# Sixteen half chunks of attention values by products of rounded halves, and the second routing search held back

## The chip, the cores and the metric

The kernel runs on one core of a Trainium2 chip. A core has a matrix engine (TensorE, PE in the rows; its weight loads are PEld), a vector engine (VectorE, DVE), a scalar engine (ScalarE, ACT), GpSimd (POOL), SyncE (SP, which only issues transfers) and 16 DMA engines. Each engine runs its own instructions in order and waits for others by semaphores. The metric is device time in microseconds (us), median of the runs; lower is better.

## The reference

A channel attention gives 20,224 tokens of 256 features, and a mixture of 8 experts with a fixed capacity works on them. Cut to what matters:

```python
qn = q / (np.linalg.norm(q, axis=1, keepdims=True) + 1e-06)      # q, k, v: 4 x 5056 x 256
kn = k / (np.linalg.norm(k, axis=1, keepdims=True) + 1e-06)
s = kn.transpose(0, 2, 1) @ qn / tau                             # 256 x 256 for each of 4 batches
a = softmax(s)                                                   # rows
x = (v @ a).reshape(20224, 256)                                  # attention values
logits = x @ w_gate                                              # 20224 x 8
for idx in np.argsort(-logits.flatten()):                        # greedy: best pairs first
    tok, e = idx // 8, idx % 8
    if assigned[tok] < 0 and counts[e] < 2528:
        assigned[tok] = e; counts[e] += 1
for e in range(8):
    out[assigned == e] = np.maximum(x[assigned == e] @ w1[e], 0) @ w2[e]
```

## The kernel before

**Stages.** First the scores of the four batches (`scores`), beside the values v @ a of batch 0 (`value`) and part of batch 1. From about 220 us PE works through the remaining values ("late" values): 13 chunks of 1024 tokens, listed in `TODO`, each in four pairs of 128 tokens (`pair` at L1494, `x_tiles` at L236). Values go through PSUM tile `px`, are evicted by ACT into `xs` (L245) and stored to the DRAM table `x_d` by a transfer that ACT issues (L251, `store_x`). Then come eight phases, one for each expert: `layer1` (L1399, tile `ph`, products at L1425) and `layer2` (L1442, tile `py`, products at L1459) over chunks of up to 512 tokens, whose rows were gathered from `x_d` by indirect transfers of POOL (L1198, tile `xg`) and turned by PE into `pt` (`turn`, `turn_both`) or by a longer way over DVE and DRAM (`stage`).

**Two kinds of product.** A late value is a matmul of full float32: per pair, 2 tiles x 2 halves of the contraction = 4 matmuls of 256 columns. Layers 1 and 2 and the values of batch 0 use three products of rounded halves instead: with v = vH + vL and a = aH + aL (H rounded to float32r, L the rest), vH aH + vH aL + vL aH, so 3 matmuls for one, in a format that PE takes in one pass.

**The routing.** Which tokens go to an expert is found by a search on DVE: `route(p, R)` prepares a 16-bit key of each token (m at L549, f at L574, the expert's one-hot `oh` at L580), then 8 rounds narrow a threshold. In a round DVE compares (`ge`, L650), PE counts (20 small matmuls, L615, and one at L628), DVE reduces, and ACT copies counts (`eq`, L643). Then `compact` and `listed` make the list of token rows: PE tests (L855, tile `pi`), ACT and DVE count them (`junk` at L873, `junkv` at L889), and DVE makes addresses (from `at`, L983, to `src`, L936). For phase 0 the list comes in two pieces, of 4 and 16 columns of 128 tokens. `("ei", 0)` in the code is the point where the expert is known (`ei`, L766), `("idx", 0)` the point where its list is complete.

**What sets the order.** From L1484 on the order is written by a planner (`Order`, L1029): the main program calls `tick` after each PE instruction with its estimated time, and `hook` then puts in DVE, PE and ACT steps of the searches where its model says that they are ready. Engines follow that order strictly. `plan` (L1119) starts the search of phase p when `("routed", p - 1)` is set, which for p = 1 lies before the list of phase 0 is complete. `pairs[:-LATE]` runs beside the first search, `until(("idx", 0))` lets the planner's clock run on (it puts nothing on PE), and the last 6 pairs stand behind it; before the sixth, four gathers and `turn_both` (L1376) bring in the first two columns of phase 0. The weights of phase 0 are loaded into `ub` when `ei` is known (L1163) and split into halves in eight pieces, `split_piece`: ACT makes the high half (L1176), DVE the low one (L1179), into the four buffers `ua`. Those four also hold values' inputs (`HOMES`); seven more chunks lie in `vr`.

## Time and profile before

| | us |
|---|---|
| time, median of 3 runs (1235.07 to 1235.74) | 1235.32 |
| the profiled execution's own time | 1232.93 |
| its span in the trace | 1231.2 |
| PE busy (98% of the span) | 1208.6 |
| DVE busy (71%) | 872.8 |
| ACT busy (46%) | 560.3 |
| POOL busy (32%) | 395.0 |
| last stretch of the late values, 307 to 322.5: PE busy of 15.5 | 15.50 |
| the list of phase 0, 290 to 307: DVE busy of 17 | 16.02 |

The profiled execution took 1232.93 us, 2.4 us less than the median. Busy time is what the profiler saw an engine execute; matmuls overlap, so a busy PE is one that has work, and what a matmul costs is read from the distance between equal steps rather than from its own duration. The timeline gives start and duration of instructions, and in brackets how long the engine had been idle and which instruction ended that wait.

### The profile page before, as it was taken

Reading aid. Unit: us, or ns where it says so; the run is one execution under the profiler, and the core shown is the slowest. Engines: PE = TensorE matmul, PEld = TensorE weight load, DVE = VectorE, ACT = ScalarE, POOL = GpSimd, SP = SyncE. Lnnn points to the kernel's source line nnn. Section 1 sums busy time; section 2 is a strip of 40 time slices with the busy share of each in tenths; the row PEclk is TensorE's granted clock in tenths of the full one; section 3 lists DMA queues with packets and bytes.
Section 4 is the critical chain, followed back from the end, with each engine's and each line's share of the span. In section 5 each row is a group of like instructions: output and inputs, shape, how many; then the busy total and the mean of one; then the engine's idle time right before and its main releaser. Section 6 shows DMA issues by size and latency. Waiting matters only on the chain.

```text
span 1231.2 us, 23522 instructions
## 1 busy us (share of the span) xinstructions
PE 1208.6 (98%) x8797; PEld 1101.6 (89%) x8797; DVE 872.8 (71%) x2414; ACT 560.3 (46%) x1301; POOL 395.0 (32%) x663
## 2 busy tenths in 40 slices
PE   7999999999999999999999999999999999999998
PEld 6889977888889999898989999989989998998998
DVE  6788695879689888979878987888766335435431
ACT  6567652235344453435343554463366435334331
POOL 1000000000353452254424443443353345344322
PEclk9999999999999999999999999999999999999999
DMA  8998985235323331332412252342243234322311
GB/s 304 357 398 310 395 322 188 103 123 204 124 95 118 113 101 66 133 95 85 148 63 87 85 184 74 116 137 90 71 148 132 78 112 166 111 81 95 115 65 34
DMA packets 67699, 179.37 MB, mean 146 GB/s; under 512 B 11008, under 2 KB 33920, under 8 KB 62976
## 3 DMA queue, kind: packets, MB, share of 16 engines
q1 hardware_dynamic: 40528, 98.58, 22.3%
q0 software_dynamic: 17664, 58.22, 14.5%
q10 hardware_dynamic: 9392, 21.06, 4.4%
q8 instruction: 69, 1.13, 0.4%
q14 instruction: 46, 0.38, 0.1%
HBM read 118.06 MB, written 59.77 MB: 144 GB/s over the span
## 4 chain that ended last, share of the span: by engine, by line
PE 81%; DVE 9%; issue 5%; POOL 2%; ACT 1%; DMA 1%; POOLq 0%; SPq 0%; DVEq 0%; ACTq 0%
PE py L1459 29%; PE ph L1425 28%; PE s L320 9%; PE px L241 8%; PE px L284 2%; PE pc L615 2%; POOL out_dram L1470 1%; PE px L432 1%; DVE hL L1434 1%; DMA xg<-x_d,src 1%; DVE acc_q L330 1%; DVE acc_k L330 1%; DVE xL L1293 1%; DMA ua<-in_q_dram 1%; DVE m L549 1%
## 5 line engine op out<-in xcount | busy, mean ns | idle before, releaser
L1459 PE MATMUL py<-ua,hH 128*128 128x256 f32 (+1 forms) x2560 | 439.2, 277 | 0.0
L1425 PE MATMUL ph<-xH,ua 128*128 128x512 f32 (+3 forms) x1312 | 395.7, 377 | 4.1 <-DVE hL L1434 3.8
L1459 PEld LDWEIGHTS py<-ua,hH 128*128 128x128 f32 (+1 forms) x2560 | 389.8, 191 | 1.4
L1459 PE MATMUL py<-ua,hL 128*128 128x256 f32 (+1 forms) x1280 | 353.1, 276 | 0.0
L1434 DVE SCALAR_TENSOR_TENSOR hL<-ph,hH 128x512 fp32r<-128x512 f32 (+3 forms) x328 | 217.7, 666 | 138.2 <-ACT hH L1429 137.5
L1429 ACT ACTIVATE hH<-ph 128x512 fp32r<-128x512 f32 (+3 forms) x328 | 190.9, 583 | 199.5 <-PE ph L1425 193.9
L1425 PEld LDWEIGHTS ph<-xH,ua 128*128 128x128 f32 x1312 | 246.3, 190 | 35.4 <-DVE hL L1434 6.9
L1470 POOL DMA_INDIRECT out_dram<-y,idx x160 | 161.8, 1011 | 305.3 <-ACT y L1468 256.2
L1425 PE MATMUL ph<-xL,ua 128*128 128x512 f32 (+3 forms) x656 | 246.9, 376 | 1.8 <-DVE xL L1293 1.8
L1459 PEld LDWEIGHTS py<-ua,hL 128*128 128x128 f32 (+1 forms) x1280 | 244.2, 191 | 0.0
L1198 POOL DMA_INDIRECT xg<-x_d,src x160 | 160.4, 1003 | 99.6 <-issue 46.9
L1468 ACT ACTIVATE y<-py 128x256 f32<-128x256 f32 (+1 forms) x160 | 61.5, 385 | 272.4 <-PE py L1459 220.8
L320 PE MATMUL s<-ua 128*128 128x256 f32 (+1 forms) x640 | 144.8, 386 | 6.9 <-DMA ua<-in_q_dram 6.9
L320 PEld LDWEIGHTS s<-ua 128*128 128x128 f32 (+1 forms) x640 | 121.8, 193 | 26.4 <-issue 10.6
L1425 PEld LDWEIGHTS ph<-xL,ua 128*128 128x128 f32 x656 | 124.9, 190 | 17.6 <-DVE xL L1293 3.9
L329 ACT ACTIVATE sq<-ua 128x1024 f32<-128x1024 f32 (+1 forms) x80 | 76.3, 970 | 49.8 <-DVE acc_k L330 16.4
L1293 DVE TENSOR_TENSOR xL<-xT,xH 128x256 fp32r<-128x256 f32 (+1 forms) x140 | 51.8, 417 | 36.6 <-ACT xH L1289 35.9
L1209 POOL COPY spacer<-hH 1x1 f32<-1x1 f32 x129 | 27.4, 212 | 154.5 <-ACT hH L1429 135.9
L245 ACT ACTIVATE xs<-px 128x512 f32<-128x512 f32 x60 | 35.8, 597 | 66.8 <-PE px L241 66.6
L350 POOL TENSOR_SCALAR ny<-ny 128x4 f32<-128x4 f32 x4 | 2.0, 505 | 182.3 <-ACT ny L349 182.3
L1179 DVE TENSOR_TENSOR ua<-ub,ua 128x512 fp32r<-128x512 f32 x64 | 47.2, 744 | 11.3 <-ACT ua L1176 9.9
L1289 ACT ACTIVATE xH<-xT 128x256 fp32r<-128x256 f32 (+1 forms) x140 | 54.2, 454 | 1.3 <-DMA xT<-via 1.3
(317 smaller groups left out, 1399.8 us busy)
## 6 DMA issues: line engine op xcount, KB each, us to landing
x_d<-xs ACTq DMA_DIRECT2D x40, 512.0 KB, 3.0
ua<-in_k_dram SPq DMA_DIRECT2D x35, 512.0 KB, 6.9
ua<-in_q_dram SPq DMA_DIRECT2D x35, 512.0 KB, 7.6
via<-xs SPq DMA_DIRECT2D x34, 512.0 KB, 2.8
xT<-via SPq DMA_DIRECT2D x136, 128.0 KB, 2.8
vr<-in_vt_dram SPq DMA_DIRECT2D x14, 1024.0 KB, 9.2
ua<-in_vt_dram SPq DMA_DIRECT2D x4, 1024.0 KB, 4.8
xg<-x_d,src POOLq DMA_INDIRECT x160
```

What stands on the lines that cost most here:

```text
L241: mm = PE.matmul(px[:, i * C:i * C + width], lhsT=vs[b, c][:, kb, t + i, :], rhs=a_f[b][:, kb, 0:width], start=(kb == 0), stop=(kb == 1))
L320: newest[0] = PE.matmul(sb[:, ib * C:(ib + 1) * C], lhsT=kt[:np_, t, ib * 128:(ib + 1) * 128], rhs=qt[:np_, t, :], start=(first and t == 0 ...
L329: S.activation(sq[:n, t0:t1], t_[:n, t0:t1], AF.Square)
L1198: P.indirect_dma_start(out=xg[:n, i, :], out_offset=None, in_=rows, in_offset=bass.IndirectOffsetOnAxis(ap=routed[p]["src", col][:n, col:c ...
L1289: S.activation(hi[:, a], rows[:, a], AF.Copy)
L1293: V.tensor_tensor(lo[:, a], rows[:, a], hi[:, a].bitcast(F32), op=OP.subtract)
L1425: PE.matmul(ph[:, 0:nt], lhsT=l[:, w], rhs=in_turn(x_, kb, nt).rearrange("p a m -> p m a"), start=(i == 0), stop=(i == 5))
L1429: S.activation(hH[:, fb, 0:nt], ph[:, 0:nt], AF.Relu)
L1434: V.scalar_tensor_tensor(hL[:, fb, 0:nt], ph[:, 0:nt], 0.0, hH[:, fb, 0:nt].bitcast(F32), op0=OP.max, op1=OP.subtract)
L1459: PE.matmul(py[:n, 0:C], lhsT=l[:, fb, tk], rhs=w, start=(j == 0), stop=(j == 23))
L1468: S.activation(y[:n], py[:n, 0:C], AF.Copy)
L1470: sd = P.indirect_dma_start(out=out, out_offset=bass.IndirectOffsetOnAxis(ap=routed[p]["idx", col][:n, col:col + 1], axis=0), in_=y[:n], i ...
```

## The change

The late chunks are divided. Five stay plain (`PLAIN`: (3,0) to (3,4)). Eight (`CLOVEN`: (2,4), (1,2) to (1,4), (2,0) to (2,3)) are worked in 16 half chunks of 512 tokens by the three products of rounded halves. For each half chunk `cleave` has ACT write -vH into the low tile (128 x 1024), POOL issue a transfer that reads v again from DRAM and adds it there (giving vL = v - vH), and ACT write vH. The halves of `a` for batches 1 and 2 are made once, the high one by ACT, the low one by POOL. `x_tiles_cut` then issues 12 matmuls for a pair. `TURNS` orders half chunks: F is two plain pairs, C one cloven half chunk; 14 plain pairs and all 32 cloven ones stand ahead of `until(("idx", 0))`, the last 6 plain ones behind it as before. `PLACES` and `BEHIND` say which freed buffer a half chunk takes and which turns must have passed. In `plan`, the search of phase 1 now waits for `("idx", 0)`. Line numbers behind the insertion are 43 to 44 higher in the changed kernel (L615 becomes L658, L549 becomes L592, L1425 becomes L1469).

```diff
@@ -67,7 +67,11 @@
 GATES_AT = (3, 3)
 FIRST_LAT = 3000
 HOMES = {(1, 0): "ub", (1, 1): "ub", (2, 4): "ua", (3, 0): "ua", (3, 1): "ua", (3, 2): "ua", (3, 3): "late", (3, 4): "late"}
-TODO = ((2, 4), (3, 0), (3, 1), (3, 2), (1, 2), (1, 3), (1, 4), (2, 0), (2, 1), (2, 2), (2, 3), (3, 3), (3, 4))
+PLAIN = ((3, 0), (3, 1), (3, 2), (3, 3), (3, 4))
+CLOVEN = ((2, 4), (1, 2), (1, 3), (1, 4), (2, 0), (2, 1), (2, 2), (2, 3))
+TURNS = "FFCFCFCCFCFCCCFCCCCCCCC"
+PLACES = ("ub", "ub", "ua", "ua", "vr", "ub", "vr", "ub", "vr", "ua", "vr", "ua", "vr", "ua", "vr", "ua")
+BEHIND = {3: "FF", 5: "C", 7: "CC", 9: "FFFF", 11: "FFFFFF", 13: "CCC", 15: "CCCC"}
 CUT = (4, 4, 4, 4, 4)
 FIRST_CUT = (2, 4, 4, 4, 4, 2)
 PE_TO_DVE = 340
@@ -511,6 +515,45 @@
             job(*j)
 
     rt = ctx.enter_context(tc.tile_pool(name="rt", bufs=1))
+    hctx = ExitStack()
+    hp = hctx.enter_context(tc.tile_pool(name="hp", bufs=1))
+    a_two = {}
+    for b in (1, 2):
+        a = a_f[b][:, :, 0:C].rearrange("p k (m a) -> p a k m", a=2)
+        h, lo = a_two[b] = [hp.tile([128, 2, 2, 128], F32R, name=f"{n}{b}") for n in ("aH", "aL")]
+        S.activation(h, a, AF.Copy)
+        P.tensor_tensor(lo, a, h.bitcast(F32), op=OP.subtract)
+
+    cloven = [(b, c, h) for b, c in CLOVEN for h in range(0, T, TH)]
+    v_cut = []
+
+    def cleave():
+        b, c, h = cloven[len(v_cut)]
+        home = PLACES[len(v_cut)]
+        y = (vp.tile([128, 2048], F32, name="vr", bufs=BUFS_V) if home == "vr" else big(home)).bitcast(F32R)
+        y = y.rearrange("p (z k n) -> p z k n", z=2, k=2)
+        raw = vs[b, c][:, :, h:h + TH].rearrange("p k t n -> p k (t n)")
+        S.activation(y[:, 1], raw, AF.Copy, scale=-1.0)
+        P.dma_start(out=y[:, 1], in_=vt[b, c].rearrange("p (k n) -> p k n", k=2)[:, :, h * 128:(h + TH) * 128],
+                    accum_op=OP.add)
+        S.activation(y[:, 0], raw, AF.Copy)
+        v_cut.append(y.rearrange("p z k (t n) -> p z k t n", t=TH))
+
+    def x_tiles_cut(k, t, xs, tick):
+        b = cloven[k][0]
+        px = next_px()
+        aH, aL = a_two[b]
+        for i in range(2):
+            j = 0
+            for kb in range(2):
+                vH, vL = (v_cut[k][:, z, kb, t + i] for z in range(2))
+                for l, r in ((vH, aH), (vH, aL), (vL, aH)):
+                    PE.matmul(px[:, i * C:(i + 1) * C], lhsT=l, rhs=r[:, :, kb].rearrange("p a m -> p m a"),
+                              start=(j == 0), stop=(j == 5))
+                    j += 1
+                    tick(112)
+        S.activation(xs[:, t:t + 2, 0:C], px.rearrange("p (t c) -> p t c", t=2), AF.Copy)
+
     ps_c = ctx.enter_context(tc.tile_pool(name="ps_c", bufs=1, space=PSUM))
     cctx = ExitStack()
     two = [cctx.enter_context(tc.tile_pool(name="two", bufs=2, space=PSUM))]
@@ -1118,7 +1161,8 @@
 
     def plan():
         p = nphase[0]
-        if p < E and done.get(("start", p)) is None and (p == 0 or done.get(("routed", p - 1))):
+        if p < E and done.get(("start", p)) is None and (
+                p == 0 or done.get(("routed", p - 1)) and (p > 1 or done.get(("idx", 0)))):
             done["start", p] = True
 
             def job(p=p):
@@ -1491,20 +1535,42 @@
         want(("ei", 0), first_w)
         rows_of = {}
 
+        def tend():
+            settle()
+            if cut_w[0] and o.pe > cut_w[0][0] and len(cut_w[0]) > 1:
+                split_piece(0, *cut_w[0].pop(1))
+
         def pair(b, c, t):
             if t % TH == 0:
                 rows_of[b, c] = x_rows()
             xs = rows_of[b, c]
             x_tiles(b, c, t, xs, C, o.tick)
-            settle()
-            if cut_w[0] and o.pe > cut_w[0][0] and len(cut_w[0]) > 1:
-                split_piece(0, *cut_w[0].pop(1))
+            tend()
             if t % TH == 2:
                 store_x(b, c, xs, t - 2, t + 2)
 
-        pairs = [(b, c, t) for b, c in TODO for t in range(0, T, 2)]
-        for at_ in pairs[:-LATE]:
-            pair(*at_)
+        pairs = [(b, c, t) for b, c in PLAIN for t in range(0, T, 2)]
+        past = ""
+        for kind in TURNS:
+            while len(v_cut) < len(cloven) and (len(v_cut) < 3 or len(v_cut) <= len(past)):
+                want_ = BEHIND.get(len(v_cut), "")
+                if any(past.count(x) < want_.count(x) for x in set(want_)):
+                    break
+                cleave()
+            if kind == "F":
+                for t in range(2):
+                    pair(*pairs.pop(0))
+            else:
+                k = past.count("C")
+                b, c, h = cloven[k]
+                xs = x_rows()
+                for t in range(0, TH, 2):
+                    x_tiles_cut(k, t, xs, o.tick)
+                    tend()
+                store_x(b, c, xs, h, h + TH)
+            past += kind
+        assert len(pairs) == LATE
+        hctx.close()
         o.until(("ei", 0))
         settle()
         o.until(("idx", 0))
@@ -1518,7 +1584,7 @@
         for c in range(2):
             load_x(0, c)
         head, queue[:] = list(queue), []
-        for n, at_ in enumerate(pairs[-LATE:]):
+        for n, at_ in enumerate(pairs):
             if n == LATE - 1:
                 queue[:] = head[:HEAD]
                 while queue:
```

What this does to the order is shown at three places.

**ACT in the first search.** `xs<-px` are evictions (L245 before; L249 plain and L555 cloven now), `eq<-pc` the copy of a round's counts, `vr<-vr` and `ub<-vr` the two writes of a half chunk. Before, the first two rounds:

```order
L245 ACTIVATE xs<-px 128x512
L643 ACTIVATE eq<-pc 128x120
L245 ACTIVATE xs<-px 128x512
L251 DMA x_d<-xs 128x1024
L245 ACTIVATE xs<-px 128x512 x2
L251 DMA x_d<-xs 128x1024
L643 ACTIVATE eq<-pc 128x120
L245 ACTIVATE xs<-px 128x512 x2
L251 DMA x_d<-xs 128x1024
```

Now, the second and third round:

```order
L255 DMA x_d<-xs 128x1024
L536 ACTIVATE vr<-vr 128x1024
L539 ACTIVATE vr<-vr 128x1024
L686 ACTIVATE eq<-pc 128x120
L555 ACTIVATE xs<-px 128x512 x2
L255 DMA x_d<-xs 128x1024
L536 ACTIVATE ub_2102<-vr 128x1024
L539 ACTIVATE ub_2102<-vr 128x1024
L555 ACTIVATE xs<-px 128x512
L686 ACTIVATE eq<-pc 128x120
```

Two writes of 128 x 1024 stand between the evictions, in three of the eight rounds just ahead of the copy of counts.

**DVE behind the list of phase 0.** `src` and `bt` end the list, `m`, `t`, `tie`, `khi`, `hi`, `klo`, `eq`, `f`, `oh` set up the second search, `ua` is a low half of weights, `xL` the low half of phase 0's first tokens. Before, from the last steps of the list:

```order
L926 TENSOR_TENSOR w__2583<-w__2583,k_2581 128x16
L928 SCALAR_TENSOR_TENSOR w__2585<-k_2584,ext 128x16
L930 SCALAR_TENSOR_TENSOR src<-k_2582,w__2583 128x16
L932 TENSOR_SCALAR early<-at 128x16
L934 TENSOR_TENSOR w__2587<-w__2585,at 128x16
L936 COPY_PREDICATED src<-early,w__2587 128x16
L580 TENSOR_TENSOR oh<-f,code_121 128x1280
L948 TENSOR_SCALAR bt<-src 128x16
L585 TENSOR_SCALAR eq<-ne_151 128x8
L951 SCALAR_TENSOR_TENSOR bt<-src,bt 128x16
L606 TENSOR_SCALAR Ex<-ne_151 32x128
```

Now, from the end of the second search's setting up to the first `xL`:

```order
L600 TENSOR_TENSOR t_3095<-t_3095,tie 128x160
L603 TENSOR_SCALAR khi<-t_3095 128x160
L606 TENSOR_SCALAR hi<-khi 128x160
L609 TENSOR_SCALAR klo<-t_3095 128x160
L612 TENSOR_TENSOR eq<-L_146,m 128x1120
L1223 TENSOR_TENSOR ua_3017<-ub_2714,ua_3016 128x512
L614 TENSOR_TENSOR eq<-eq,code_121 128x1120
L1223 TENSOR_TENSOR ua_3017<-ub_2714,ua_3016 128x512
L617 TENSOR_REDUCE f<-eq 128x160
L619 TENSOR_TENSOR f<-f,U_147 128x160
L623 TENSOR_TENSOR oh<-f,code_121 128x1280
L1433 TENSOR_TENSOR xL<-pt,xH 128x2x128 x2
```

The eleven steps from `m` to the second `f` that lay among the steps of the list have moved behind `idx`, with two of the eight low halves of weights; `xL` of the first tokens stands behind `oh`.

**PE from the last late pairs to layer 1.** `pt<-identr,xg` turns the first tokens, `pc<-oh,ge` and `pc<-Ex,ones_q` are counts of a search, `pi` the last test of phase 0's list. Before:

```order
L615 LDWEIGHTS ge
L615 MATMUL pc<-oh,ge 128x64
L241 MATMUL px<-a_last,vr_1573 128x256
L1384 MATMUL pt<-identr,xg 128x128 x4
L241 MATMUL px<-a_last,vr_1573 128x256 x3
L628 MATMUL pc<-Ex,ones_q 128x128
L241 MATMUL px<-a_last,vr_1573 128x256
L1425 MATMUL ph<-xH,ua_2565 128x256
```

Now:

```order
L898 LDWEIGHTS G
L898 MATMUL pi<-E__97,G 128x162
L551 MATMUL px<-aH_1800,ua_2580 128x256
L551 MATMUL px<-aL_1801,ua_2580 128x256
L551 MATMUL px<-aH_1800,ua_2580 128x256
L245 MATMUL px<-a_last,vr_1571 128x256 x8
L245 MATMUL px<-a_last,vr_1573 128x256 x12
L1428 MATMUL pt<-identr,xg 128x128 x4
L245 MATMUL px<-a_last,vr_1573 128x256 x4
L1469 MATMUL ph<-xH,ua_2886 128x256
L1469 MATMUL ph<-xL,ua_2886 128x256
```

The two rounds of the second search that stood among the last six pairs have moved behind the start of layer 1; between the last test and the turn stand 20 plain matmuls.

## Rows read from the trace of the kernel before

**Rows 1.** The page, parts 5 and 6: a group's mean ns; transfers.

```profile
L329 ACT ACTIVATE sq<-ua 128x1024 f32<-128x1024 f32 (+1 forms) x80 | 76.3, 970 | 49.8 <-DVE acc_k L330 16.4
...
ua<-in_q_dram SPq DMA_DIRECT2D x35, 512.0 KB, 7.6
```

**Rows 2.** Busy us per engine in two stretches, clock, DMA share, GB/s.

```profile
290.00:307.00 17.00, 15.58 (x82) 13.18 (x82) 16.02 (x42) 12.46 (x37) 0.00 (x0) 1.00 0.39 158
...
307.00:322.50 15.50, 15.50 (x110) 13.67 (x109) 10.81 (x43) 5.71 (x11) 4.10 (x4) 1.00 0.47 169
```

**Rows 3.** Timeline of ACT (start, us, instruction): two evictions.

```profile
203.91 0.60 ACT L245 ACTIVATE xs<-px 128x512 f32<-128x512 f32 x1 [1.13 <-PE px L241]
205.64 0.60 ACT L245 ACTIVATE xs<-px 128x512 f32<-128x512 f32 x1 [1.13 <-PE px L241]
```

**Rows 4.** Chain that ended last: start, us, piece.

```profile
340.08 2.72 DMA xg<-x_d,src
...
1036.76 10.72 PE py L1459 x96
```

**Rows 5.** Timeline, one round of the first search.

```profile
263.85 1.48 DVE L650 TENSOR_TENSOR ge<-low,thr 128x1200 bf16<-128x1200 int16 x2
...
265.87 0.75 PE L615 MATMUL pc<-oh,ge 128*128 128x64 bf16 x20
...
266.46 1.54 PE L241 MATMUL px<-a,vr 128*128 128x256 f32 x6
...
267.65 0.41 PE L628 MATMUL pc<-Ex,ones_q 128*128 128x128 f32 x1
...
267.89 3.24 PE L241 MATMUL px<-a,vr 128*128 128x256 f32 x14
```

**Rows 6.** Timeline of DVE, the searches and the list of phase 0.

```profile
221.78 2.40 DVE L549 TENSOR_REDUCE m<-L 128x160 f32<-128x1280 f32 x1
...
231.49 1.49 DVE L580 TENSOR_TENSOR oh<-f,code 128x1280 bf16<-128x1280 f32 x1
...
279.67 0.15 DVE L766 SCALAR_TENSOR_TENSOR ei<-es,pcol 128x1 int32<-128x1 f32 x1
...
290.48 2.08 DVE L549 TENSOR_REDUCE m<-L 128x160 f32<-128x1120 f32 x1
...
307.67 0.16 DVE L983 TENSOR_SCALAR at<-sgn 128x9 int32<-128x9 f32 x1
...
308.88 0.18 DVE L936 COPY_PREDICATED src<-early,w__2587 128x16 int32<-128x16 int32 x1
```

**Rows 7.** Timeline of ACT while the second list is made.

```profile
294.00 0.39 ACT L873 ACTIVATE junk<-pi,rhalf 128x160 bf16<-128x160 f32 x1 [0.23 <-PE pi L855]
...
298.21 0.60 ACT L245 ACTIVATE xs<-px 128x512 f32<-128x512 f32 x1 [0.42 <-PE px L241]
298.70 0.62 ACT L1176 ACTIVATE ua<-ub 128x512 fp32r<-128x512 f32 x1
```

**Rows 8.** Timeline from the list to layer 1.

```profile
311.13 1.47 DVE L650 TENSOR_TENSOR ge<-hi,th 128x1200 bf16<-128x1200 int16 x2
...
311.47 1.26 POOL L1198 DMA_INDIRECT xg<-x_d,src  x1 [28.91 <-DVE bt L951]
...
315.54 0.95 POOL L1198 DMA_INDIRECT xg<-x_d,src  x1 [0.30 <-issue]
...
322.52 0.42 DVE L1389 TENSOR_TENSOR xL<-pt,xH 128x256 fp32r<-128x256 f32 x1 [0.45 <-ACT xH L1388]
...
322.55 0.46 PE L1425 MATMUL ph<-xH,ua 128*128 128x256 f32 x1
```

**Rows 9.** Timeline of PE after a long wait; two stretches there.

```profile
621.84 0.48 PE L1425 MATMUL ph<-xH,ua 128*128 128x512 f32 x1 [2.26 <-DVE hL L1434]
...
620.00:624.00 4.00, 2.16 (x7) 1.56 (x8) 3.89 (x14) 0.53 (x2) 0.00 (x0) 0.88 0.19 60
624.00:628.00 4.00, 4.00 (x30) 3.10 (x29) 3.79 (x15) 1.37 (x4) 0.36 (x2) 0.70 0.00 0
```

## Prediction

> **What bounds the kernel now.** I read the engines' busy time by stretch first. In the last stretch of the late values PE is busy all 15.5 us; while the list of phase 0 is made, just before, DVE is busy 16.02 of 17 us and PE 15.58 [rows 2]. So two things run nose to nose from 220 to 322 us: PE with 52 pairs of values, and the chain search, list, gather. Then I read how far apart evictions of px are where nothing else is between: 203.91 to 205.64, so a pair costs PE 1.73 us [rows 3], and the chain of waits, where 96 matmuls of layer 2, three products of rounded halves over 256 columns, take 10.72 us, 0.112 us each [rows 4]. Layer 1 begins at 322.55 [rows 8]; all that follows is a chain of PE work, so the change is worth what it moves that moment, plus what it moves across it.
>
> **The change part by part.**
>
> *Matmuls.* A cloven pair is 12 x 0.112 = 1.34 us instead of 1.73, 0.39 less; 32 pairs save 12.3 us of PE. That is the ceiling. Nothing of it counts unless the list is earlier too, because `turn_both` needs gathered tokens.
>
> *First search.* Its 8 rounds keep their steps. A round's counts cost PE 0.59 us (265.87 to 266.46) and 0.24 us (267.65 to 267.89) [rows 5] and stand behind whatever matmul runs. A plain matmul is 0.43 us, a cloven one 0.11, so the mean wait for it falls from 0.22 to 0.06, 0.16 for each of 16 visits, 2.5 us at most; those among plain turns gain nothing, so I take 1.0. `ei`, at 279.67 + 0.15 [rows 6], comes at about 278.8.
>
> *ACT.* A half chunk adds two writes of 128 x 1024. The trace has such an instruction of another kind, 0.97 us [rows 1], so 1.94 us for 16 half chunks, three of them ahead of the first search. A cloven turn then costs ACT 1.94 + 2 x 0.60 = 3.1 us beside 2.7 us of PE and about half a round's counts (0.4 us), a plain turn 3.1 beside 3.5 + 0.6: even on the mean, up to 2 us behind at times. With four px buffers PE can run three pairs ahead (4 to 5 us), which hides it; where a copy of counts stands behind two writes DVE may wait some tenths. Bounds: 0 to 3 us on the search; I take 0, the planner's spacing leaving the writes room.
>
> *Transfers.* Sixteen of 512 KB, each read from DRAM and added in place; none such is in the trace. Nearest are plain loads of 512 KB, landing 7.6 us after issue (median, under the heavy traffic of the scores) [rows 1]. Half chunks have at least four turns of lead, 11 us and more. Bounds: free up to 11 us each, from there PE waits. POOL, which issues them, is idle there; the copies cost it a few tenths to 1.4 us each, going by its gathers [rows 8]. Free is the nearer bound.
>
> Beside those gathers the comparison on DVE took 1.47 us for two (311.13) [rows 8], and 1.48 with POOL idle (263.85) [rows 5]: no lengthening. The Trainium skill, "SBUF — State Buffer", section "Who interferes with whom", says that VectorE in its two-port modes and GpSimd writing descriptors shut each other out, which would speak against issuing 16 transfers beside a search. The rows show it for this comparison not at all; by the rule the short DVE steps that use such modes could wait up to one issue each, which stays in the 3 us above.
>
> *The list of phase 0.* Today 279.82 to 309.06, 29.2 us [rows 6], DVE nearly full [rows 2]. Taken out of it are the second search's eleven steps up to `f`. The first search took 11.2 us from `m` (221.78) to the end of `oh` (231.49 + 1.49) with eight experts [rows 6]; without `oh` 9.7, with seven about 8.5. Two low halves of weights go too, 1.3 us (an estimate from ACT's 0.62 for the same tile [rows 7]). DVE alone would then need 29.2 - 9.8 = 19.4 us. But ACT becomes the later one. Its first test follows `m` today at 294.00 [rows 7]; without `m` (2.08 us) and 1.0 earlier, at 290.9. Then in ACT's order: nine tests of 0.39, four evictions of 0.60, four high halves of 0.62, three small copies (0.2): 9.0 us, and about 1.5 us of waiting for PE's pairs, which come 1.34 us apart: 301.4. Addresses take DVE 1.4 us (307.67 to 309.06) [rows 6]: `src` at 302.8, **6.3 us earlier**. Bounds: 299.6 (DVE alone) and 306 (ACT 3 us behind).
>
> *From the list to layer 1* there are three branches.
> PE: 322.55 - 12.3, less two rounds of the second search that are gone from here (2 x 0.83): 308.6, the sixth pair included.
> Gathers: four issues take 311.47 to 316.49; a gather on the chain lasted 2.72 us from issue to landing [rows 4, 8]. From 302.8 + 0.5 the last lands at 310.0, and one pair stands behind the turn: 312.3.
> DVE: `idx` 0.7 us, then the held-back search from `m` to `oh`, about 10.1, with two low halves among it 1.3: 314.9. Only then come the two `xL` of 0.42 us with ACT's high half between them, 1.3 us in all: 316.2, where today the second ends at 322.94 [rows 8].
> DVE is the last: layer 1 starts in earnest about **6.6 us earlier**. What was taken from the list stands in front of `xL` instead; `idx` needs it less than layer 1 does.
>
> *What crosses the border.* The two rounds are done behind it now: 1.7 us of PE. The changed order sends one more chunk of phase 0 over PE's turns instead of DRAM (8 transposes and their stalls, taken as 0.6 us). Net 4.3 us.
>
> *Clock.* PE would idle some 3 us ahead of the turn and some 4 ahead of layer 1. After a wait of 2.26 us at 619.6, the granted clock fell to the lower of its two levels, 1.2 GHz, for a while: means of 0.88 and 0.70 over two stretches of 4 us, 1.7 us lost [rows 9]. Here part of it falls where PE waits anyway. Bounds 0 and 1.7 (twice that if both waits do it); I take 0.5.
>
> *Sum:* 6.6 - 1.7 - 0.6 - 0.5 = 3.8 us. The profiled execution's 1232.93 would be 1229.1; it was 2.4 us below the median, so against the median 1235.32 it gives **1231.5**. The later phases are the same work in a slightly different order: a single PE wait there can be 2.26 us long [rows 9], so 2 us either way is allowed for.
>
> **Rivals.**
>
> *PE's gain arrives almost whole.* If ACT finishes the list as early as DVE would allow (299.6) and `oh` with it, layer 1 starts near 313, 9.5 us early, without a wait long enough for the clock: 9.5 - 2.3 = 7.2, time 1228. With PE alone as the bound, 12.3 + 1.7 - 2.3 = 11.7 less, 1223.6. For it: lengths on ACT are taken without overlap. Against: `oh` stands before `xL` in any case.
>
> *It comes to nothing.* ACT is 3 us behind when the tests begin and the clock falls twice: 6.6 - 3 - 2.3 - 1.7 is about zero, 1233 to 1237.
>
> *Slower: the adding transfers are slow.* They all go through POOL's queue, and so do the weights of phase 0 behind them. If one takes over about 5 us of the DMA engines (sixteen in some 70 us), the backlog grows past the lead, PE waits for low halves, and the weights land late, so ACT stops at their high halves with evictions and tests behind them. At 7 us each the last would be some 30 us late against a lead of about 25; 5 us of PE and the 4 us of gain gone: 1240. For it: nothing like these is in the trace; against it: DMA is busy 0.39 and 0.47 in these stretches [rows 2].
>
> *The products are not cheap.* If a cloven matmul were bound by its weight load and cost 0.19 us, a pair would take 2.3 us, 18 us more in all and some 1242 after PE's slack. Layer 2 changes weights with every matmul and keeps 0.112 [rows 4], so it is unlikely.
>
> **How the numbers follow.** Forecast 0.45, most of PE's gain 0.17, nothing 0.20, slow transfers 0.13, dear products 0.05. A measurement of this kernel tells apart about 0.2%, 2.5 us, so faster means below 1232.9. The forecast's own range, 1228.5 to 1234, lies 0.39 below that and 0.06 within; with 0.17 above it faster is 0.56; same is 0.06 and 0.19 of the third case, 0.25; the rest, 0.19, is slower. The range 1224.5 to 1237.5 leaves the two slow rivals and the extreme of the second out.
>
> **What would show it.** Right: evictions of cloven pairs 1.34 us apart; `ei` near 279; the second search's `m` behind `idx`, `src` near 303; a PE gap before the turn and one before layer 1, ended by `xL`; layer 1 near 316. Wrong: a PE wait ended by a POOL transfer, rounds longer than before, ACT waiting for weights, layer 1 bound by gathers or starting before 314, or phases 1 to 7 changing length by more than 2 us.

## The result, and the profile after

| | before | after |
|---|---|---|
| time, median of 6 runs each, us | 1234.68 (1233.13 to 1235.74) | 1245.13 (1242.01 to 1248.84) |
| ratio, 95% interval | | 1.0085 (1.0067 to 1.0104) |
| span of the profiled execution | 1231.2 | 1243.3 |
| first eviction of layer 1 (`hH`) | 324.33 | 327.06 |
| from there to the last eviction of layer 2 (`y`) | 902.30 | 909.03 |
| from there to the end of the span | 4.5 | 7.2 |

The changed kernel is 10 us slower, where 4 us less were forecast. The last three lines divide the 12.1 us between the spans: layer 1 starts 2.7 later instead of 6.6 earlier, the phases last 6.7 longer instead of 2.3, and 2.7 lie behind the last eviction, where I expected nothing. The trace of before is of an execution 1.8 us below the median of its 6, that of after of one at its median, so some 2 of the 12.1 us are scatter of single runs.

**What went as forecast.** Timeline of ACT: evictions of cloven pairs, and the first high half of the weights.

```profile
288.32 0.60 ACT L555 ACTIVATE xs<-px 128x512 f32<-128x512 f32 x1 [0.37 <-PE px L551]
...
289.66 0.60 ACT L555 ACTIVATE xs<-px 128x512 f32<-128x512 f32 x1 [0.17 <-PE px L551]
...
291.00 0.60 ACT L555 ACTIVATE xs<-px 128x512 f32<-128x512 f32 x1 [0.74 <-PE px L551]
...
299.80 0.63 ACT L1220 ACTIVATE ua<-ub 128x512 fp32r<-128x512 f32 x1 [6.86 <-DMA ub<-in_w1t_dram,ei]
```

The pairs are 1.34 us apart, against 1.73 [rows 3]: the products are as cheap as worked out. The last row is the first thing that is not: ACT stood 6.86 us for the weights.

**The DMA engines.** Busy time by stretch (PE, PEld, DVE, ACT, POOL, granted clock, DMA share, GB/s), then the software queue's line of the page (packets, MB, share of 16 engines' span) and the stores of values (median us to landing). First the kernel before in the same stretches, then the changed kernel:

```profile
240.00:270.00 30.00, 30.00 (x245) 26.57 (x244) 23.65 (x82) 10.44 (x21) 0.00 (x0) 1.00 0.34 137
270.00:300.00 30.00, 28.33 (x164) 24.04 (x163) 26.48 (x108) 13.54 (x36) 2.14 (x2) 1.00 0.54 197
...
x_d<-xs ACTq DMA_DIRECT2D x40, 512.0 KB, 3.0
```

```profile
240.00:270.00 30.00, 29.79 (x307) 28.12 (x306) 23.93 (x81) 25.56 (x40) 8.66 (x8) 1.00 1.03 248
270.00:300.00 30.00, 27.38 (x250) 26.38 (x246) 21.56 (x98) 16.32 (x30) 5.31 (x5) 1.00 1.07 316
300.00:320.00 20.00, 17.01 (x85) 14.98 (x85) 14.69 (x50) 13.73 (x40) 3.85 (x4) 0.83 0.46 166
```

```profile
q0 software_dynamic: 22016, 66.61, 18.1%
...
x_d<-xs ACTq DMA_DIRECT2D x40, 512.0 KB, 7.1
```

From 240 to 300 us the DMA engines are full (1.03 and 1.07, where the kernel before had 0.34 and 0.54; the share adds up the times of all packets, so packets that overlap on an engine carry it past 1), and a store takes 7.1 us instead of 3.0.

**The chain to layer 1.** One piece of the chain that ended last, DVE's timeline, and what PE waited for between 280 and 345 us (total, times, longest):

```profile
283.75 16.02 DMA ub<-in_w1t_dram,ei
```

```profile
223.65 2.44 DVE L592 TENSOR_REDUCE m<-L 128x160 f32<-128x1280 f32 x1
226.12 1.16 DVE L595 TENSOR_SCALAR t<-m 128x160 f32<-128x160 f32 x1
227.32 1.22 DVE L598 TENSOR_SCALAR tie<-t 128x160 int32<-128x160 int32 x1
...
282.71 0.15 DVE L809 SCALAR_TENSOR_TENSOR ei<-es,pcol 128x1 int32<-128x1 f32 x1
...
312.80 0.18 DVE L979 COPY_PREDICATED src<-early,w__2911 128x16 int32<-128x16 int32 x1
...
313.74 2.10 DVE L592 TENSOR_REDUCE m<-L 128x160 f32<-128x1120 f32 x1
...
323.48 1.49 DVE L623 TENSOR_TENSOR oh<-f,code 128x1280 bf16<-128x1280 f32 x1
324.89 0.42 DVE L1433 TENSOR_TENSOR xL<-pt,xH 128x256 fp32r<-128x256 f32 x1
```

```profile
PE ph L1469 <- DVE xL L1433: 5.3, 1, 5.3
PE pi L898 <- DVE ext L935: 4.6, 1, 4.6
```

`m` comes 1.9 us later than in [rows 6], `ei` 3.0, `src` 3.9. Two short steps behind `m` took 1.16 and 1.22 us. In the kernel before they took 0.24 each, and ACT's first high half of the weights came 10.2 us behind their issue (280.1):

```profile
224.21 0.24 DVE L552 TENSOR_SCALAR t<-m 128x160 f32<-128x160 f32 x1
224.49 0.24 DVE L555 TENSOR_SCALAR tie<-t 128x160 int32<-128x160 int32 x1
...
290.27 0.62 ACT L1176 ACTIVATE ua<-ub 128x512 fp32r<-128x512 f32 x1
```

Now the weights needed 16 us, the list stood behind ACT's high halves, and PE waited 4.6 us. Then the second search ran from `m` to `oh` in front of `xL`, and PE waited 5.3 us more. Behind either wait the clock fell; busy time by stretch again:

```profile
300.80:307.60 6.80, 4.71 (x24) 4.62 (x25) 4.42 (x18) 4.71 (x15) 0.00 (x0) 0.50 0.41 164
...
324.70:331.50 6.80, 6.14 (x42) 5.90 (x43) 4.32 (x12) 2.02 (x5) 1.63 (x2) 0.50 0.22 84
```

Granted clock 0.50 is the lower level, 1.2 GHz, 6.8 us each time; half of what PE was busy there, 2.4 and 3.1 us, was lost.

### The profile page after: what moved, and what is told of

It is laid out like the page before. It is cut to its first block, busy times and chain, and to the rows that moved or that the text cites. A ratio compares the mean times of both kernels' runs of the same rounds, so it can differ in the third digit from the quotient of the medians.

```text
span 1243.3 us, 23860 instructions
## 1 busy us (share of the span) xinstructions
PE 1204.9 (97%) x8933; PEld 1100.4 (89%) x8933; DVE 876.0 (70%) x2410; ACT 588.6 (47%) x1333; POOL 417.6 (34%) x681
## 4 chain that ended last, share of the span: by engine, by line
PE 73%; DVE 12%; issue 6%; ACT 3%; DMA 3%; POOL 2%; SPq 0%; ACTq 0%; POOLq 0%; DVEq 0%
PE py L1503 28%; PE ph L1469 26%; PE s L324 9%; PE px L288 2%; PE pc L658 2%; PE px L245 2%; DVE hL L1478 2%; PE px L436 1%; DMA ub<-in_w1t_dram,ei 1%; POOL out_dram L1514 1%; PE px L551 1%; DVE ua L1223 1%; DVE m L592 1%; DVE f L617 1%; DVE acc_q L334 1%
## 5 line engine op out<-in xcount | busy, mean ns | idle before, releaser
L1469 PE MATMUL ph<-xH,ua 128*128 128x512 f32 (+3 forms) x1312 | 395.9, 377 | 3.5 <-DVE hL L1478 3.4
L1469 PEld LDWEIGHTS ph<-xH,ua 128*128 128x128 f32 x1312 | 245.7, 191 | 34.6 <-DVE hL L1478 6.5
L1469 PE MATMUL ph<-xL,ua 128*128 128x512 f32 (+3 forms) x656 | 247.4, 377 | 7.4 <-DVE xL L1433 5.3
L1469 PEld LDWEIGHTS ph<-xL,ua 128*128 128x128 f32 x656 | 125.2, 191 | 24.6 <-DVE xL L1433 5.8
L1253 POOL COPY spacer<-hH 1x1 f32<-1x1 f32 x129 | 30.6, 237 | 155.2 <-ACT hH L1473 141.2
L1223 DVE TENSOR_TENSOR ua<-ub,ua 128x512 fp32r<-128x512 f32 x64 | 47.2, 744 | 19.4 <-ACT ua L1220 18.5
L334 DVE TENSOR_TENSOR acc_k<-acc_k,sq 128x1024 f32<-128x1024 f32 (+2 forms) x40 | 44.3, 1112 | 12.0 <-ACT sq L333 10.3
```

The costliest lines, as they stand in the source:

```text
L334: V.tensor_tensor(acc[:n, t0:t1], acc[:n, t0:t1], sq[:n, t0:t1], op=OP.add)
L1223: e.tensor_tensor(lo, raw, h.bitcast(F32), op=OP.subtract)
L1469: PE.matmul(ph[:, 0:nt], lhsT=l[:, w], rhs=in_turn(x_, kb, nt).rearrange("p a m -> p m a"), start=(i == 0), stop=(i == 5))
```

## The experiments

Seventeen experiments ran, on four chips (1 to 8, 9 to 11, 12 to 14, 15 to 17). The kernel before took 1234 us on the first (experiments 1 to 8) and 1240 to 1242 on the others (9 to 17), so each is held against before on its own chip (the trace of before shown ahead took 1232.93 us, as on the first). The changed kernel was measured earlier, beside a before of 1234.7 us; a difference to it is 1.1 us smaller by the ratios than by the times. "Start" is the first eviction of layer 1, "phases" from there to the last eviction of layer 2, "behind" from there to the end of the span; these three are from one profiled execution each, and kernels that run the same code up to `m` of the first search differ there by up to 1.2 us (221.8 before, 222.9 in 2). 9 and 10 ran once, so they have no interval.

| kernel | us | ratio to before, interval | start | phases | behind |
|---|---|---|---|---|---|
| before (first chip) | 1234.0 | | 324.3 | 902.3 | 4.5 |
| after | 1245.1 | 1.0085 (1.0067, 1.0104) | 327.1 | 909.0 | 7.2 |
| 1 not held back | 1240.1 | 1.0053 (1.0040, 1.0066) | 331.0 | 899.2 | 7.2 |
| 2 before, held back | 1238.1 | 1.0035 (1.0022, 1.0048) | 325.3 | 905.9 | 4.4 |
| 3 weights apart | 1245.5 | 1.0096 (1.0078, 1.0113) | 325.1 | 911.6 | 7.2 |
| 4 no transfers | 1237.6 | 1.0033 (1.0019, 1.0047) | 320.5 | 910.8 | 4.4 |
| 5 no transfers, not held back | 1230.7 | 0.9973 (0.9964, 0.9983) | 325.5 | 899.1 | 4.5 |
| 6 plain transfers | 1237.8 | 1.0035 (1.0021, 1.0048) | 320.2 | 908.2 | 6.1 |
| 7 low halves by POOL | 1258.6 | 1.0198 (1.0184, 1.0212) | 351.5 | 899.3 | 4.5 |
| 8 twelve half chunks | 1236.8 | 1.0023 (1.0014, 1.0032) | 330.1 | 900.0 | 6.2 |
| 9 halves of a by DVE | 1253.4 | 1.0093 | 326.6 | 917.5 | 7.2 |
| 10 one transfer | 1239.9 | 0.9984 | 320.6 | 913.0 | 4.4 |
| 11 eight half chunks | 1237.2 | 0.9958 (0.9946, 0.9970) | 323.9 | 905.5 | 5.4 |
| 12 eight, held back | 1245.3 | 1.0036 (1.0024, 1.0048) | 321.1 | 914.3 | 5.4 |
| 13 another order of before | 1239.2 | 0.9992 (0.9983, 1.0001) | 325.1 | 908.7 | 4.5 |
| 14 another order of before | 1240.0 | 1.0000 (0.9987, 1.0013) | 327.0 | 907.9 | 4.5 |
| 15 before (another chip) | 1240.3 | 0.9995 (0.9983, 1.0006) | 325.5 | 911.6 | 4.5 |
| 16 eight half chunks | 1236.9 | 0.9972 (0.9960, 0.9983) | 323.3 | 905.7 | 5.4 |
| 17 eight, no transfers | 1236.9 | 0.9965 (0.9954, 0.9977) | 326.1 | 904.6 | 4.5 |

**1 and 2: the held-back search.** Undone in the changed kernel (1), made alone in the kernel before (2):

```diff
-        if p < E and done.get(("start", p)) is None and (
-                p == 0 or done.get(("routed", p - 1)) and (p > 1 or done.get(("idx", 0)))):
+        if p < E and done.get(("start", p)) is None and (p == 0 or done.get(("routed", p - 1))):
```

> The changed kernel with the search of phase 1 started as before, not held back behind the list of phase 0. Theory B (the held-back search stands in front of xL): in the changed kernel PE waits 5.3 us for xL while DVE does m to oh, and then runs 6.8 us at half clock. With the search started early its steps fall into the 5.6 us that DVE idles for the weights; the list itself still waits for the weights, so src stays near 313, xL comes at 319 to 320, the second clock fall goes. 5.3 + 3, less what DVE adds to the list: 1236 to 1239. Theory A (the late weights alone): the list bounds everything, xL moves less than 2 us, 1243 to 1246.

> The kernel before with only the search of phase 1 held back behind the list of phase 0; nothing else changed. As DVE was full while the list was made, src should come 5 to 6 us earlier (303) and xL behind oh, near 317, before PE is through its pairs (320.9, two rounds of counts being gone). Forecast from that: layer 1 is 1.7 us earlier and two rounds later in the phases, 1234 to 1236, no difference. Theory B in a strong form (a later second search delays phase 1 and so on): 1237 to 1240. If the gain of the list arrives elsewhere: under 1232.

Both say that holding back costs: 5.0 us in the changed kernel (3.9 by the ratios), 4.0 in the kernel before. But not where I had put it; 1240.1 is also above the range of theory B. With the search freed, layer 1 starts 4 us later (331.0), as DVE has its steps among the list again (`src` 317.9); the gain is in the phases, 899.2 instead of 909.0. In the kernel before the list did get shorter, from 29.2 to 26.1 us between `ei` (280.82 here) and `src`, and the phases longer, from 902.3 to 905.9:

```profile
306.89 0.18 DVE L936 COPY_PREDICATED src<-early,w__2583 128x16 int32<-128x16 int32 x1
```

Where in the phases it lies can be read from the last eviction of `y` in each. Held back, the first five phases take 123.0, 118.3, 117.0, 116.0 and 114.9 us in the changed kernel, freed (1) 118.9, 115.8, 116.0, 114.6 and 114.1; the last three are equal. In the first phase part of it is the second stretch at half clock, which lies ahead of layer 1 in experiment 1, and one more round of counts. The six later searches end 3.5 to 10.7 us later (`ei`), and PE is idle for 10.9 us of the phases instead of 5.9; 11.3 instead of 8.7 in the kernel before. That the later searches cause this waiting is argued from these numbers, not shown by an experiment of its own.

**3: the weights apart from POOL's queue.**

```diff
+        if p == 0:
+            nc.sync.dma_start(out=raws[p, i], in_=(w1t, w2t)[i][0:128])
+            return
         P.indirect_dma_start(out=raws[p, i], out_offset=None, in_=(w1t, w2t)[i],
```

> The changed kernel with the weights of phase 0 loaded by SyncE's plain transfers (always those of expert 0, so the output of that phase is not the reference's) and not by POOL's queue behind the adding transfers. Theory A (weights behind the transfers): PE's wait of 4.6 us, DVE's of 5.6 and the first clock fall (300.8 to 307.6, 3.4 us lost) go, src comes at 305 to 307, xL, six us earlier as DVE is, at 318 to 319: 1236 to 1239. If A is wrong and the list is late for other reasons (ACT behind with its writes): src stays at 311 to 313, 1243 to 1246.

No change in time: the theory fell in this form. What was waited for between 284 and 316 us (total, times, longest):

```profile
ACT xs L555 <- DMA x_d<-xs: 5.4, 4, 2.2
PEld px L551 <- DMA ua<-in_vt_dram: 3.4, 2, 1.8
PE px L551 <- DMA ua<-in_vt_dram: 3.0, 2, 1.6
...
PE px L551 <- DMA vr<-in_vt_dram: 1.4, 1, 1.4
```

The weights were no longer late, but PE now waited for low halves and ACT for stores. So the place in the queue is not what costs most, but that the DMA engines are full (1.05 and 1.07 here): whoever is not late makes another late. Layer 1 did start 2.0 us earlier (325.1); the phases took that back, in part by a stretch at half clock at 738 us that the changed kernel does not have.

**4 and 6: no transfers, and plain ones.** Experiment 4 leaves `P.dma_start` in `cleave` out; experiment 6:

```diff
-                    accum_op=OP.add)
```

> The changed kernel without the 16 adding transfers: the low tile stays the negative of the high half, so the attention values of 16 half chunks are wrong; the searches see the same logits, everything else is the same work. Theory A: as with the weights apart, 1236 to 1239, and what it is below that one is what the transfers cost beside the weights (stores that take 7.1 us instead of 3.0, POOL's 1.1 us for each). If the transfers were free, as I had predicted: 1243 to 1246.

> The changed kernel with plain instead of adding transfers: the same bytes from the same queue, but v is written over the low tile instead of added to it, so the values of 16 half chunks are wrong. If adding is what makes them dear: DMA engines busy well under 1.0 between 240 and 300, weights landing within 11 us, 1236 to 1239. If it is the traffic of any such transfer: as the changed kernel, 1243 to 1246. The end tells the same for POOL's last drain: 3.2 us if adding makes it long, 6 us if any of these transfers does.

Without the transfers the kernel is 7.5 us faster, and with plain ones of the same bytes 7.4 (6.4 and 6.2 by the ratios): it is the adding that is dear. With plain ones ACT's first high half of the weights came 9.1 us behind their issue. The software queue's line of 4, then of 6; and from 240 us on the stretches of 6:

```profile
q0 software_dynamic: 17664, 58.22, 14.4%
```

```profile
q0 software_dynamic: 22016, 66.61, 16.8%
```

```profile
240.00:270.00 30.00, 29.77 (x306) 28.10 (x305) 24.37 (x82) 25.70 (x40) 5.71 (x8) 1.00 0.83 276
270.00:300.00 30.00, 28.75 (x261) 27.80 (x260) 25.25 (x110) 20.76 (x43) 4.17 (x5) 1.00 0.84 299
```

The 16 transfers are 4352 packets. Adding, they took 0.181 x 1243.3 - 0.144 x 1235.6 = 47 us of 16 engines, 0.173 us a packet and 2.9 us a transfer; plain, 0.168 x 1234.5 less the same 177.9, 29 us, 0.108 a packet and 1.8 a transfer. Adding ones were issued some 3.5 us apart, and stores and loads filled 0.36 of the engines in that stretch of experiment 4, so 2.9 / 3.5 + 0.36 = 1.19 is over 1, and 1.8 / 3.5 + 0.36 = 0.87 is not. That full engines alone lengthened the adding packets is ruled out by the eight transfers of experiment 16 against none in 17: 0.166 x 1234.3 - 0.145 x 1235.2 = 26 us, 3.2 each, at a DMA share of 0.78.

Experiment 4 also shows the forecast's middle part undisturbed: `src` of the list and PE's waits between 300 and 345 us.

```profile
305.83 0.18 DVE L977 COPY_PREDICATED src<-early,w__2895 128x16 int32<-128x16 int32 x1
```

```profile
PE ph L1467 <- DVE xL L1431: 6.0, 1, 6.0
PE pt L1403 <- DMA xg<-x_d,src: 1.6, 1, 1.6
```

From `ei` (281.82) to `src` it is 24.0 us, as worked out, and ACT's tests end it, as forecast; the wait for `xL` stands there as well.

**5: the products alone.** Experiments 1 and 4 in one.

> Products of halves alone: the changed kernel without the adding transfers (the low tile stays the negative of the high half, so 16 half chunks of values are wrong) and with the search of phase 1 started early, as before. Theory now: three costs stand against a good gain, the transfers' share of the DMA engines (the changed kernel against the one without them: 8 us), the held-back search (the kernel before with it alone: 4 us slower), and 2.8 us that POOL's last drain lasts longer in all kernels with adding transfers. Taken both out: layer 1 near 321, phases as short as in the kernel with only the search freed (899 us from the first to the last eviction of a layer), end 4.5 behind: 1226 to 1230. Rival: the products gain nothing, as DVE sets the time of the list anyway: 1233 to 1236.

1230.7, just above the range. With low halves for nothing the kernel is 3.3 us faster than before, but layer 1 does not start earlier (325.5): DVE sets it, `ei` (282.75) and `src` (311.98) are 3 us late, and PE's saving is spent waiting. The longest of its waits between 220 and 345 us:

```profile
PE pc L656 <- DVE ge L691: 6.6, 4, 4.4
```

The gain is in the phases, and it is not shown to be the products'. The third phase takes 115.8 us instead of 119.5, as the wait of [rows 9] and its stretch at half clock are gone, which is more than the 3.3. Experiment 7, whose layer 1 starts 26 us later, has the same phases (899.3). Holding back costs 6.9 us here (4 against 5).

**7: low halves by POOL**, not held back.

```diff
-        S.activation(y[:, 1], raw, AF.Copy, scale=-1.0)
-        P.dma_start(out=y[:, 1], in_=..., accum_op=OP.add)
         S.activation(y[:, 0], raw, AF.Copy)
+        P.tensor_tensor(y[:, 1], raw, y[:, 0].bitcast(F32), op=OP.subtract)
```

> The low halves made by POOL as v minus the high half (an instruction of 128x1024 for each of 16 half chunks, about 2.5 us going by the 2.54 that the halves of a took), no transfers, ACT's negative copy gone; the search of phase 1 started early. If POOL's instructions only lie beside the search: 1226 to 1230, as without transfers. If they lengthen DVE's steps as beside the halves of a (a step of 0.24 us took 1.16 there, the next one 1.22): two or three such steps in each of 8 rounds, 0.9 each, the search 10 to 20 us longer, 1238 to 1250.

Worse than expected, 25 us. Timelines of DVE and of POOL there:

```profile
258.35 3.65 DVE L691 TENSOR_TENSOR ge<-hi,thr 128x1200 bf16<-128x1200 int16 x2
```

```profile
258.69 2.66 POOL L537 TENSOR_TENSOR vr<-vr 128x1024 fp32r<-128x1024 f32 x1 [1.76 <-ACT vr L536]
```

The comparison, 1.48 us with POOL idle [rows 5], took 3.65 beside POOL's subtraction. `ei` came at 308.9. With 1258.6 us it lies above the upper range too.

**9: the halves of a by DVE.** In the changed kernel POOL makes these halves just when DVE does the two slow steps; its timeline, then the edit:

```profile
223.70 2.23 POOL L1060 MEMSET ge<- 128x2560 bf16 x1 [3.00 <-DVE L L441]
225.90 2.54 POOL L525 TENSOR_TENSOR aL<-a,aH 128x512 fp32r<-128x512 f32 x2
```

```diff
-        P.tensor_tensor(lo, a, h.bitcast(F32), op=OP.subtract)
+        V.tensor_tensor(lo, a, h.bitcast(F32), op=OP.subtract)
```

> The changed kernel with the low halves of a (two subtractions of 128x512) made by DVE, behind m, and not by POOL. In the changed kernel the two steps behind m, 0.24 us each in the kernel before, took 1.16 and 1.22 while POOL made these halves. If POOL's instruction held them up: 0.24 each, DVE does two more of about 0.7, m to oh 0.5 us shorter than 11.66. If they were long for another reason (code, DMA): still over 1 us each. The total is not told apart by this.

DVE's timeline in it:

```profile
226.93 0.23 DVE L595 TENSOR_SCALAR t<-m 128x160 f32<-128x160 f32 x1
227.19 0.24 DVE L598 TENSOR_SCALAR tie<-t 128x160 int32<-128x160 int32 x1
```

So POOL's instruction had held them up, 1.9 us, and `m` to `oh` is 10.85 us instead of 11.66. The Trainium skill, "SBUF — State Buffer", section "Who interferes with whom", says that VectorE in a two-port mode contends with GpSimd, and VectorE with two SBUF inputs contends with a GpSimd instruction that reads SBUF: whichever issues first holds the shared ports for its whole instruction, and the other is blocked. Experiments 7 and 9 agree with it: 0.24 became 1.16 for a step with one input, 1.48 became 3.65 for a pair of comparisons with two inputs each; which mode a step ran in, no row shows. The one run took 1253.4 us, 0.9% above its before, as the changed kernel did; the total tells nothing here, as expected.

**8 and 11: fewer half chunks, not held back.** Twelve and eight, the rest plain (8 pairs more for each four), with a list of the turn from which each may be cleaved; 11 also has the edit of 9.

```diff
-TURNS = "FFCFCFCCFCFCCCFCCCCCCCC"
+TURNS = "FFCFCFCFCFCFCFCFCFFFFFF"
+AT = (0, 0, 0, 3, 5, 7, 9, 11)
```

> Twelve half chunks instead of sixteen ((2,2) and (2,3) stay plain), their adding transfers spread so that the last is issued some 20 us ahead of the weights; the search of phase 1 started early. Theory (too many transfers in too short a time): PE saves 9.4 us instead of 12.3, DMA stays under 0.9, the weights land in 10 us, list src near 311, 1230 to 1233 with the 2.8 us of the last drain in it. Rival (every adding transfer costs its share wherever it lies): three quarters of the loss of the sixteen, 1236 to 1239.

> An attempt at a faster kernel: eight half chunks by products (chunks (2,4), (1,2), (1,3), (1,4)), their adding transfers spread with about two turns between, the halves of a by DVE, the search of phase 1 started early. PE saves 6.2 us. With 24 us of DMA engines for eight transfers in some 55 us the engines are not full, the weights land in 10 us, the list is bound by DVE as in the kernel before: layer 1 at 323 to 326, phases 899 to 902 as in the other kernels with the search started early, 5.5 behind: 1230 to 1233. Rival (the products bring nothing where DVE sets the list, and each transfer costs): 1234 to 1238.

Twelve came out in the rival's range, but the theory is not refuted by it: the last transfer was issued at 287.3, not 20 us ahead of the weights but right in front of them. POOL had stood for it, and so the weights behind it were issued 3.9 us after `ei` (284.80 to 288.72), against 0.9 in the changed kernel (282.86 to 283.75); PE waited 4.9 us and layer 1 started at 330.1. Here the place in POOL's order did hold the weights up. Eight, whose last transfer is issued at 264, beat the kernel before by 0.42%.

**10: what the end goes by.**

```diff
-        P.dma_start(out=y[:, 1], in_=...
+        if not v_cut:
+            P.dma_start(out=y[:, 1], in_=...
```

> The changed kernel with the first adding transfer alone; the other 15 are left out, so 15 half chunks of values are wrong. It tells what POOL's last drain goes by. From the last eviction to the end it is 4.4 us without transfers, 6.1 with 16 plain ones, 6.2 with 12 adding ones, 7.2 with 16 adding ones. If it goes by their number: 4.5 to 4.7. If one is enough: 6 to 7.3.

Last eviction and span, of the kernel before, of after and of experiment 10:

```profile
core 0 of [0], span 1231.2 us
...
1226.63 0.38 ACT L1468 ACTIVATE y<-py 96x256 f32<-96x256 f32 x1 [2.24 <-PE py L1459]
```

```profile
core 0 of [0], span 1243.3 us
...
1236.09 0.38 ACT L1512 ACTIVATE y<-py 96x256 f32<-96x256 f32 x1 [2.24 <-PE py L1503]
```

```profile
core 0 of [0], span 1238.0 us
...
1233.57 0.38 ACT L1513 ACTIVATE y<-py 96x256 f32<-96x256 f32 x1 [2.23 <-PE py L1504]
```

4.5, 7.2 and 4.4 us. Nearly all of the difference is one instruction at the end of POOL's program, a drain: 3.16 us in the trace of before, 6.04 in that of after. One transfer costs nothing there, eight 0.9, twelve 1.7, sixteen plain ones 1.6 and sixteen adding ones 2.7. It grows with their number and their kind; why POOL's last drain does so, a thousand microseconds later, is open.

**12 to 14: held back again, and the order alone.** 12 is 11 with the search held back. 13 and 14 are the kernel before with `FIRST_LAT`, the modelled start of DVE, at 4500 and 6000 instead of 3000.

> The kernel with eight half chunks (its transfers do not fill the DMA engines and it was 0.42% faster than before), with the search of phase 1 held back again as in the changed kernel. If holding back costs by itself (4.0 us in the kernel before, 5.0 in the changed one, 6.9 without transfers): 4 to 7 us slower than with the search started early, 0 to 0.2% above the kernel before. If it cost only where PE was ahead of DVE by all 16 half chunks: within 2 us of the eight, still 0.3 to 0.4% below before.

> The kernel before with one number of its planner changed (the modelled start of DVE, 4500 ns instead of 3000), so that the same steps stand in another order from the first search to phase 6. It tells how much of the differences behind the start of layer 1 may be the order alone. If the order alone matters by as much as 3 us: from the first to the last eviction of a layer 899 to 906 us instead of 902.3, the total 3 us to either side. If not: within 1 us of 902.3 and of the kernel before.

> The same with 6000 ns instead of 3000, a second sample of the order. The wait of 2.26 us at 621.8 in the kernel before, and the clock fall behind it, are from its order: if either of the two samples is without it, its phases are some 2.9 us shorter there.

Holding back costs again: 1.0036 against 0.9958 and 0.9972, 8 to 10 us, more than expected; layer 1 starts 2 to 3 us earlier and the phases are 9 longer. The two other orders are the same as before in time, within 0.2%. Their phases (908.7 and 907.9) are in neither range expected, but tell nothing by themselves, as there is no trace of before from that chip; two samples do not bound what another order can bring.

**15 to 17: where the eight gain.**

> The kernel before itself, unchanged, so that there is a trace of it from the same chip as the next two. The chips differ: it took 1234 us beside the first eight experiments and 1240 to 1242 beside the later ones. Expected: 1.000 of the kernel before; where its layer 1 starts and how long its phases are is what the next two are held against.

> The kernel with eight half chunks, the search started early, once more, beside a trace of the kernel before from the same chip. 0.995 to 0.997 of before. If the products bring it, layer 1 starts 2 to 5 us earlier than in the kernel before. If the order brings it, layer 1 starts within 1 us of it and the phases are 3 to 5 us shorter.

> The eight half chunks without their adding transfers (the low tiles stay the negative of the high halves, so eight half chunks of values are wrong). Eight transfers that do not fill the DMA engines should cost only POOL's last drain: 0.9 us less than with them (5.4 against 4.5 behind the last eviction). If adding transfers cost beyond that even so: 2 to 5 us less.

On one chip the eight start layer 1 2.2 us earlier (323.3 against 325.5) and their phases are 6.0 shorter (905.7 against 911.6); 0.9 goes behind the last eviction. These are 7.3 us between two single executions, where the medians are 3.4 apart: the trace of before is of a run 3.2 us above its median. The start is not steady either: without their transfers (17) the eight start at 326.1, later than before, with the same time in all (1236.9). PE's waits between 440 and 660 us, of the kernel before and of the eight:

```profile
PE ph L1425 <- DVE hL L1434: 3.9, 2, 2.9
PE ph L1425 <- issue: 1.6, 2, 1.3
```

```profile
PE pt L899 <- DVE ext L1014: 1.0, 1, 1.0
PE ph L1469 <- issue: 0.9, 1, 0.9
PE ph L1469 <- DVE hL L1478: 0.7, 2, 0.5
```

The kernel before has the wait of [rows 9] there, 2.9 us in this run, with its stretch at half clock; the eight do not. That wait is gone in orders 13 and 14 too, and those are no faster; in order 13 another wait, 1.8 us at 672 us, has a stretch at half clock behind it. So the eight are 0.3 to 0.4% faster, on two chips, but that this is the products' doing is not shown: neither rival of experiment 16 came out alone. Without their transfers the eight are as fast as with them (0.9965 against 0.9972): where the DMA engines are not full (0.78 from 240 to 270 us), adding costs nothing that can be told from the scatter.

## Why the prediction was wrong, point by point

*Matmuls, 12.3 us saved:* right, 1.34 us a pair. But no run shows that time arriving: held back and without transfers (4) layer 1 starts 3.9 us earlier, and not held back (5) no earlier at all.

*First search, 1.0 less:* right in its own steps, wrong in sum. From the end of `oh` to `ei` it is 45.9 us instead of 46.7, 0.8 less. But POOL's halves of `a` held DVE up 1.9 us ahead of it. I had weighed POOL beside DVE for its issues alone, by a row in which POOL issues gathers, and had costed the two subtractions on POOL at nothing. The issues themselves did no harm: of 39 steps of this search that ran beside one, a single one is longer than in experiment 4, by 0.2 us. And `m` itself came 1.9 us later; the same steps of before have it at 222.9 in experiments 2 and 15, the changed ones at 222.8 to 223.7 in 1, 4, 5 and 6, so most of that is scatter of single runs.

*ACT, 0 taken of 0 to 3:* its writes took 1.05 us instead of 0.97. No row shows DVE waiting longer for counts but one of 0.63 us. Right.

*Transfers, "free is the nearer bound":* this step failed, and it is the larger part. I took the price from landing times of plain loads; what counts is engine time, 2.9 us for each. The rival of slow transfers had the place right and the threshold wrong: I put the tipping point at 5 us of engine time, which would be right for 16 in 80 us with nothing else (in the 70 us named there it is 4.4), and had the 0.39 and 0.47 of other traffic in [rows 2] before me. Its mechanism, weights behind transfers in one queue, is not the main one: experiment 3 took it out and was no faster, so full engines are enough. Cost: 7.5 us (6.4 by the ratios), of which 2.8 lie at the end of the program, which no case had.

*The list, 24.0 us from `ei` to `src`:* right without transfers (24.0), 30.1 with them. ACT was the later one, as forecast; that it agrees to a tenth is luck, as ACT's first test came 1.2 us later behind `ei` than worked out and the rest took 1.1 less. The lower bound of 299.6 does not follow from its own terms: 278.8 + 19.4 is 298.2.

*The held-back search, "`idx` needs it less than layer 1 does":* right that `xL` would be last and PE wait for it (5.3 us, forecast some 4). The two rounds and the 8 transposes did cross the border as counted (160 instead of 120 count matmuls of 64 columns, 48 instead of 40 transposes). Wrong that this 2.3 us was all: I took the later searches as unmoved, and they end 3.5 to 10.7 us later than with the search freed, with PE idle for 5 us more of the phases. Alone the holding back costs 4.0 us in the kernel before and 4 to 10 in the others, where it was to gain. Second failed step; how the later searches turn into PE's waits is not taken apart.

*Clock, 0.5 taken of 0 to 3.4:* mis-sized. Both waits did it, and each fall lasted 6.8 us where that of [rows 9] cost 1.7 us: 2.4 and 3.1 us lost, 5.5 in all and above the bound. How much of the first lies in time in which PE would have waited anyway is not taken apart.

*Later phases, "2 us either way":* mis-sized, for the same reason as the held-back search. With it started early they take 899 to 902 us on one chip, held back 906 to 912.

In sum, the two big terms explain the result: taking both out (5) moves the kernel from 10 us above the one before to 3.3 below. That this is near the 3.8 forecast is luck: layer 1 starts no earlier there, and a wait in the third phase that is gone, with its stretch at half clock, is worth as much.

## What to carry to other kernels

Cost a transfer by the engine time of its packets, add the DMA share that the stretch already has, and treat a sum over 1 as a wait for everything that is loaded or stored there; here 1.19 made loads and stores late (a store 7.1 us instead of 3.0), and 0.87 hardly did (3.9). Where two engines run nose to nose, a saving on one of them is worth what the other can follow; of 12 us of PE at most 4 reached the start of layer 1, and no run shows a shorter time that is certainly theirs. Work taken out of a full stretch must be costed where it lands, with all that is chained to it.

## What was not expected of the hardware

An adding packet of 1.9 KB took 0.173 us of a DMA engine, a plain one from the same queue 0.108 (after and experiment 6, against 4). POOL's last drain lengthens by up to 2.7 us with transfers issued a thousand microseconds before. A POOL subtraction that reads SBUF held DVE's short steps from 0.24 to 1.2 us, and a comparison from 1.48 to 3.65. The same kernel took 1234 us on one chip and 1240 to 1242 on three others, with most of the difference between two traces in the phases (902.3 against 911.6, the second of a run 3.2 us above its median).
